# A banded attention and gated scan kernel on one core: a new due-time list schedule, copies moved from DMA to engines, weights loaded on 128 partitions, a second PSUM home for the finals

## The chip, the cores and the metric

The kernel runs on one core of one Trainium2 chip. The metric is the device time of one execution, in microseconds (us). A run here is one execution; medians and ranges are over several. A run is called slow when it is over 1.5% above the fastest of the same kernel, and comparisons use fast runs. Before: 215.98 us median of 4 runs (215.73 to 220.17, the last a slow run) in the comparison with the changed kernel.

Engine names in the profile: PE is TensorE (PEld its weight loads), DVE is VectorE, ACT is ScalarE, POOL is GpSimd, SP is SyncE, which here issues all DMAs but one of 2 KB from one queue (SPq), one after another in its timeline.

## The reference, cut to what matters

```python
# q, k, v: 8 batches x 8 heads x 576 x 64, f32
scores = (q @ k.T) / 8                       # only |i - j| <= 32 counts
attn   = softmax(where(band, scores, -1e9))
x      = heads_side_by_side(attn @ v)        # 8 x 576 x 512
proj   = x @ w_in                            # w_in 512 x 1024
val, gate = proj[..., :512], proj[..., 512:]
for t in range(576):                         # a scan along the sequence
    h = exp(A_log)[0] * h + val[:, t];  ys[:, t] = h
out = (gate * sigmoid(gate) * ys) @ w_out    # w_out 512 x 512
```

## The kernel before

The kernel cuts the 4608 rows (8 x 576) into 9 chunks of 512. Each chunk has 4 attention steps (one for each pair of heads, so 36 steps), then 4 `val` and 4 `gate` projections with scan, tanh, silu and fuse, then 4 finals. The names below return in the profile: `sc` scores, `probs` exp and mask, `pv` probabilities times v, `xT` the transposed attention output, `pjv` and `pjg` the projections, `h` the scan, `fu` the product, `fo` a final, `osb` its eviction (the copy out of PSUM, the memory that the matmuls here write), `tr` the transposes of q and k. I call the PSUM buffer that a result goes to its home.

Nothing is ordered by hand. A small list scheduler, run while the program is written, has a duration and a due time for each of 818 pieces. It picks the engine that can start first and on it, among the pieces that could start within a slack, the one with the earliest due time:

```python
TAU = 4.0
PENALTY = {("pool", "dve"): 1.0, ("pool", "act"): 1.2, ("act", "dve"): 0.3, ("dve", "pool"): 1.0}
SLACK = 0.3
# ... cut: place(k) gives the earliest start and the engine of a piece
while ready:
    cand = [(p[1], ops[k][2], k, p) for k in ready for p in [place(k)] if p]
    cand.sort(key=lambda x: x[0])
    s0, _, _, p0 = cand[0]
    _, _, k, (_, s, d, e) = min((x for x in cand if x[3][3] == p0[3] and x[0] <= s0 + SLACK),
                                key=lambda x: x[1])
    # ... cut: bookkeeping
    emit(e)

# a due time, by a hand-made pattern of 4 us a step:
add(("norm", t), do_norm, dict(dve=0.95), t0 + TAU + 1.2, [("P", t)], opens=[("x16", t)], uses=[("pv", t)])
```

v is needed twice: in blocks that start at even multiples of 64 (`vE`) and at odd ones (`vO`), which is `vE` with the two halves of the partitions exchanged. From the third batch on `vO` is filled by two DMAs from SBUF to SBUF. The weights `w_in` come in by DMAs of 64 partitions each, since that gives the row order that `xT` has:

```python
def shift_v(b, half):
    E, O = vEs[b % 3], vOs[b % 3]
    if half == 0:
        nc.sync.dma_start(out=O[0:64].rearrange("p e h d -> p (e h d)"),
                          in_=E[64:128, 0:4].rearrange("p e h d -> p (e h d)"))
    else:
        nc.sync.dma_start(out=O[64:128].rearrange("p e h d -> p (e h d)"),
                          in_=E[0:64, 1:5].rearrange("p e h d -> p (e h d)"))

src = moe_w_in.rearrange("(s f d) (g c) -> s d f g c", s=2, f=4, g=2)
for s in range(2):
    for g in range(2):
        eng.dma_start(out=t[64 * s:64 * s + 64, :, g, :], in_=src[s, :, :, g, 256 * i:256 * i + 256])

def final(c, tt):
    fo = ps.tile([128, 2, 512], f32, tag="sc", name="fo", bufs=1)[:, 0, :]   # one PSUM home, shared with sc
```

The program keeps one PSUM buffer each for `tr`, `sc` and `pv`, and one of half that size each for `pjv` and `pjg`; finals borrow that of `sc`.

The softmax here doesn't subtract the row's maximum and nothing guards it: scores larger than these inputs give would overflow.

Of the kernel before, what the change touches and what calls it, by code (L numbers as in the profile page):

```python
# [12 lines left out]
TAU = 4.0  # L13
PENALTY = {("pool", "dve"): 1.0, ("pool", "act"): 1.2, ("act", "dve"): 0.3, ("dve", "pool"): 1.0}


def p_all(ns, b, batches):
    return [t for t in range(ns) if b >= 0 and b in batches(t // 4)]


class Sched:
# [4 lines left out]
    def __init__(self):  # L26
        self.ops, self.bufs, self.users = {}, {}, {}
# [4 lines left out]
    def add(self, key, emit, engines, due, deps, opens=(), uses=(), lock=0, mode=None, dma=0.0):  # L32
        self.ops[key] = (emit, engines, due, deps, opens, lock, mode, dma)
        for u in {*opens, *uses}:
            self.users.setdefault(u, []).append(key)

    def run(self):
        ops, users = self.ops, self.users
        left = {k: len(set(o[3])) for k, o in ops.items()}
        after = {}  # L40
        for k, o in ops.items():
            for d in set(o[3]):
                after.setdefault(d, []).append(k)
# [3 lines left out]
        self.log = []  # L47

        def place(k):
            emit, engines, due, deps, opens, lock, m, dma = ops[k]  # L50
            t = max([end[d][0] + (0.12 if end[d][1] != "pe" else 0.2) for d in deps if not (dma and ops[d][7])], default=0.0)
            for u in opens:
                o, n = opened[u[0]], self.bufs[u[0]]
                if len(o) >= n:
                    for x in users[o[len(o) - n]]:
                        if x not in end:
                            return None
                        t = max(t, end[x][0] + 0.1)
            best, first = None, next(iter(engines))
            for e, d in engines.items():  # L60
                s = max(t, free.get(e, 0.0))
                if lock and e in ("dve", "pool") and port[1] != e:
                    s = max(s, port[0])
                if e == "pe" and m != mode[0]:
                    d = d + 0.095
                c = s + d + (PENALTY.get((first, e), 0.0))
                if best is None or c < best[0]:
                    best = (c, s, d, e)
            return best

        while ready:
            cand = [(p[1], ops[k][2], k, p) for k in ready for p in [place(k)] if p]
            cand.sort(key=lambda x: x[0])
            s0, _, _, p0 = cand[0]
            _, _, k, (_, s, d, e) = min((x for x in cand if x[3][3] == p0[3] and x[0] <= s0 + SLACK),
                                        key=lambda x: x[1])
            emit, engines, due, deps, opens, lock, m, dma = ops[k]
            ready.remove(k)
            free[e] = s + d
            end[k] = (s + d, e)  # L80
            if e == "pe":
                mode[0] = m
            if lock and e in ("dve", "pool"):
                port[:] = [s + d, e]
            if dma:
                chan[0] = max(chan[0], s + 0.3) + dma
                end[k] = (chan[0] + 1.2, e)
                free[e] = max(s + d, chan[0] - 6.0)
            for u in opens:
                opened[u[0]].append(u)  # L90
            self.log.append((s, d, e, k))
            emit(e)
            for n in after.get(k, ()):
                left[n] -= 1
                if not left[n]:
                    ready.append(n)
        assert len(end) == len(ops)


SLACK = 0.3  # L100

# [3 lines left out]
def kernel(  # L105
# [23 lines left out]

    stage = {}  # L130
# [21 lines left out]
    def load_w(i, eng):  # L152
        t = T([128, 4, 2, 256], f32, "w32", bufs=2)
        src = moe_w_in.rearrange("(s f d) (g c) -> s d f g c", s=2, f=4, g=2)
        for s in range(2):
            for g in range(2):
                eng.dma_start(out=t[64 * s:64 * s + 64, :, g, :],
                              in_=src[s, :, :, g, 256 * i:256 * i + 256])
        stage["w", i] = t

    def cast_w(i, j):
        t = stage["w", i]
        for g in range(2):
            c0 = 512 * g + 256 * i + 128 * j
            nc.gpsimd.tensor_scalar(
                out=w_in16[:, :, c0:c0 + 128], in0=t[:, :, g, 128 * j:128 * j + 128],
                scalar1=1.0, scalar2=1.0, op0=ALU.mult, op1=ALU.mult)
# [6 lines left out]
    def cast_wo(a):  # L174
        nc.gpsimd.tensor_scalar(out=w_out16[:, 2 * a:2 * a + 2, :], in0=stage["wo"][:, 2 * a:2 * a + 2, :],
                                scalar1=0.5, scalar2=1.0, op0=ALU.mult, op1=ALU.mult)
# [43 lines left out]
    def cast(en, o, i):  # L220
        if en == "act":
            nc.scalar.activation(o, i, AF.Copy, bias=0.0, scale=1.0)  # L222
        elif en == "dve":
            nc.vector.tensor_copy(o, i)  # L224
        else:
            nc.gpsimd.tensor_scalar(out=o, in0=i, scalar1=1.0, scalar2=1.0, op0=ALU.mult, op1=ALU.mult)
# [4 lines left out]
    def shift_v(b, half):  # L231
        E, O = vEs[b % 3], vOs[b % 3]
        if half == 0:
            nc.sync.dma_start(out=O[0:64].rearrange("p e h d -> p (e h d)"),
                              in_=E[64:128, 0:4].rearrange("p e h d -> p (e h d)"))
        else:
            nc.sync.dma_start(out=O[64:128].rearrange("p e h d -> p (e h d)"),
                              in_=E[0:64, 1:5].rearrange("p e h d -> p (e h d)"))
# [117 lines left out]
    def final(c, tt):  # L356
        fo = ps.tile([128, 2, 512], f32, tag="sc", name="fo", bufs=1)[:, 0, :]
# [23 lines left out]
    def eng(e):  # L381
        return {"dve": nc.vector, "act": nc.scalar, "pool": nc.gpsimd, "sp": nc.sync}[e]

# [4 lines left out]
    for k, n in dict(k32=4, q32=4, k16=2, q16=2, w32=2, tr=1, sc=1, pv=1, pjv=1, pjg=1, probs=2, x16=2,  # L388
                     xT=2, th=2, silu=2, fu=2, osb=4, h0=2, h1=2, h2=2, h3=2).items():
        tag(k, n)  # L390
# [18 lines left out]
    prev = None  # L409
    for i, k in enumerate(order):  # L410
        due = 0.01 * i
        deps = [prev] if prev else []
        if k[0] == "ld":
            _, b, g, n = k
            due = max(due, TAU * (4 * b + 2 * g - 9))
            add(k, lambda en, b=b, g=g, n=n: load_qk(b, g, n, nc.sync), dict(sp=0.5), due, deps,
                opens=[(n + "32", b, g)], dma=2.0)
        elif k[0] == "ldv":
            _, b, e = k
            due = max(due, TAU * (4 * b - 8))  # L420
            deps += [("ve", b - 2, j) for j in range(5)] + [("vo", b - 2, j) for j in range(4) if b < 4] if b > 1 else []
            add(k, load_e(b, e), dict(sp=0.5), due, deps, dma=1.2)
        elif k[0] == "ldw":
            add(k, lambda en, i=k[1]: load_w(i, nc.sync), dict(sp=2.0), due, deps, opens=[("w32", k[1])], dma=3.5)
        else:
            add(k, lambda en: load_wo(), dict(sp=0.5), due, deps, opens=[("w32", 2)], dma=3.5)
        prev = k

    for i in range(2):
        for j in range(2):  # L430
            add(("cw", i, j), lambda en, i=i, j=j: cast_w(i, j), dict(pool=1.3), TAU * (4 + i), [("ldw", i)],
                uses=[("w32", i)], lock=1)
        add(("cwo", i), lambda en, i=i: cast_wo(i), dict(pool=1.1), TAU * 7, [("ldo",)], uses=[("w32", 2)], lock=1)
    for cc in range(4):
        add(("arep", cc), lambda en, cc=cc: prep_a(cc), dict(act=1.0), TAU * 3.5 + 0.1 * cc, [("exp", 1)])
    add(("arep0",), lambda en: nc.vector.memset(arep[:, :, 512:513], 0.0), dict(dve=0.1), TAU * 4,
# [4 lines left out]

    for b in range(B):
        for g in range(2):
            for o, n in enumerate("kq"):
                k, t0 = (b, g, n), TAU * (4 * b + 2 * g - 2 + o)
                add(("c",) + k, lambda en, k=k: cast_qk(*k, en), dict(pool=1.25, dve=0.8, act=1.15),
                    t0 - 2 * TAU, [("ld",) + k], opens=[(n + "16", b, g)], uses=[(n + "32", b, g)], lock=1)

                def do_T(en, k=k):
                    live[("tr",) + k] = trans(*k)  # L450

                add(("T",) + k, do_T, dict(pe=0.28), t0 + 0.3, [("c",) + k], opens=[("tr",) + k],
                    uses=[(n + "16", b, g)], mode="row")
                add(("E",) + k, lambda en, k=k: evac(k[0], k[1], live.pop(("tr",) + k), k[2]), dict(act=1.1),
                    t0 + 1.2, [("T",) + k] + ([("S", t) for t in s_steps(b - 2, g)] if b > 1 else []),
                    uses=[("tr",) + k])
        for e in range(5):
            add(("ve", b, e), lambda en, b=b, e=e: cast_v(b, e, e + 1, en), dict(pool=0.65, dve=0.45, act=0.6),
                TAU * (4 * b - 4 + 0.7 * e), [("ldv", b, e)] + ([("P", t) for t in p_all(NS, b - 3, batches)]), lock=1)
# [118 lines left out]
```

## Time and profile before

| | before |
|---|---|
| median of 4 runs | 215.98 us |
| profiled span | 216.7 us |
| TensorE busy | 166.7 us |
| last load of q landed | 146.1 us |
| exp of steps 10, 11, 12 (from 1) | 55.0, 76.0, 79.1 us |

The profiled run took 218.62 us, 2.6 us more than the median. It counts as fast, but all times within this trace come from a long run.

The profile page of the kernel before: span, busy time of each engine, then the span in 40 equal slices (each digit is tenths of busy time; PEclk is the granted TensorE clock), then the chain of work that ended last, by engine.

```profile
span 216.7 us, 5582 instructions
PE 166.7 (77%) x2304; PEld 88.3 (41%) x2304; DVE 131.4 (61%) x217; ACT 140.9 (65%) x190; POOL 115.6 (53%) x126
...
PE   0215649885398478999898999978999999999851
...
PEclk9999999998569958999999999996999999999999
DMA  5999999988999999998998998998112122122232
...
PE 37%; DMA 32%; SPq 12%; ACT 7%; DVE 4%; POOL 4%; issue 3%; POOLq 1%; ACTq 0%; DVEq 0%
```

The DMA row is full up to slice 28 (150 us) and nearly empty after it; the PE row has holes up to about slice 16 (90 us).

Busy time of each engine in three stretches of the kernel before (columns: stretch, its length, PE, PEld, DVE, ACT, POOL busy with the number of instructions, granted clock, DMA share, GB/s):

```profile
0.00:20.00 20.00, 3.75 (x109) 3.22 (x111) 4.74 (x30) 11.85 (x15) 12.27 (x20) 1.00 1.01 228
20.00:90.00 70.00, 50.07 (x756) 28.31 (x752) 38.33 (x59) 46.04 (x57) 47.58 (x53) 0.88 1.00 254
90.00:216.70 126.70, 112.91 (x1447) 56.78 (x1446) 88.33 (x129) 83.01 (x119) 55.77 (x54) 0.99 0.58 175
```

TensorE idles 16.3, 19.9 and 13.8 us in them (length less busy).

The timeline of TensorE in the kernel before (start, length, instruction; in brackets the idle time before it and what ended it):

```profile
58.21 0.66 PE L251 MATMUL tr<-ident,k_892 64*128 64x64 f16 x18 [3.27 <-POOL k_892 L226]
58.81 0.61 PE L310 MATMUL pv<-ident,x_915 128*128 128x128 f16 x4
59.21 1.91 PE L359 MATMUL fo<-w_out_64,fu 128*128 128x512 f16 x4
60.92 1.91 PE L324 MATMUL pjv<-xT,w_in_63 128*128 128x512 f16 x4
...
64.20 1.02 PE L324 MATMUL pjv<-xT,w_in_63 128*128 128x512 f16 x4
...
75.53 0.22 PE L292 MATMUL pv<-vO_94,probs 128*64 128x65 f16 x1 [3.06 <-DMA vO_94<-vE_91]
```

And SyncE's queue at that time:

```profile
53.15 10.72 SPq L144 DMA_DIRECT2D v_1_68<-in_v_dram  x5
...
65.13 0.53 SPq L234 DMA_DIRECT2D vO_94<-vE_91  x1
```

`vO` for batch 3 is issued at 65.1 us, behind five v loads that held the queue for 10.7 us, and TensorE waits for it until 75.5 us. The first four lines show something else: four matmuls of a projection take 1.91 us at 60.9 us and 1.02 at 64.2. The clock records of this trace give 0.5 from 52.6 to 62.9, 76.5 to 83.4 and 148.2 to 151.6 us. These stretches last 10.2, 6.8 and 3.4 us. The three stretches in the windows view (columns as above):

```profile
52.60:62.90 10.30, 6.49 (x74) 3.55 (x76) 3.06 (x6) 4.26 (x6) 8.61 (x10) 0.50 1.08 298
76.50:83.40 6.90, 5.72 (x94) 3.88 (x96) 4.06 (x8) 4.65 (x6) 4.90 (x5) 0.51 0.91 169
148.20:151.60 3.40, 3.40 (x24) 1.40 (x23) 2.90 (x6) 1.90 (x3) 1.47 (x1) 0.50 0.82 248
```

The last finals of the kernel before:

```profile
208.05 1.02 PE L359 MATMUL fo<-w_out_64,fu 128*128 128x512 f16 x4 [0.69 <-ACT osb L222]
209.81 1.02 PE L359 MATMUL fo<-w_out_64,fu 128*128 128x512 f16 x4 [0.73 <-ACT osb L222]
```

With one home each final waits for the eviction of the one before.

### The profile page before, as it was taken

How to read it: one execution, taken by the hardware profiler on the slowest of the kernel's cores; microseconds unless marked ns; L12 is line 12 of the kernel's file. 1: busy time of each engine (PE TensorE's matmuls, PEld its weight loads, DVE VectorE, ACT ScalarE, POOL GpSimd, SP SyncE). 2: the span in 40 equal slices, each digit the busy share in tenths (PEclk: the TensorE clock that was granted, in tenths of full speed). 3: DMA queues.
4: the chain of work that ended last, by engine and by line, in shares of the span. 5: the costliest groups of instructions: out<-in, count | busy, mean ns of one | idle time of the engine just before them, and what ended most of it. 6: DMA issues, size and time to landing. Idle time of an engine off the chain costs nothing.

```text
span 216.7 us, 5582 instructions
## 1 busy us (share of the span) xinstructions
PE 166.7 (77%) x2304; PEld 88.3 (41%) x2304; DVE 131.4 (61%) x217; ACT 140.9 (65%) x190; POOL 115.6 (53%) x126
## 2 busy tenths in 40 slices
PE   0215649885398478999898999978999999999851
PEld 0104534434234254444545545443555444444310
DVE  5004354568328464677598968846787888876600
ACT  2498897747356175688958777756679576644521
POOL 7653672599879663563758493764222423324410
PEclk9999999998569958999999999996999999999999
DMA  5999999988999999998998998998112122122232
GB/s 140 261 296 216 273 270 224 317 201 221 375 167 273 284 178 263 281 263 224 318 343 191 257 342 214 253 294 279 52 50 99 48 77 74 48 97 97 100 142 101
DMA packets 55609, 44.45 MB, mean 205 GB/s; under 512 B 39456, under 2 KB 41504, under 8 KB 55584
## 3 DMA queue, kind: packets, MB, share of 16 engines
q1 hardware_dynamic: 55056, 44.10, 74.6%
q8 instruction: 18, 0.29, 0.6%
q10 hardware_dynamic: 528, 0.00, 0.1%
q14 instruction: 7, 0.06, 0.1%
HBM read 31.46 MB, written 9.44 MB: 189 GB/s over the span
## 4 chain that ended last, share of the span: by engine, by line
PE 37%; DMA 32%; SPq 12%; ACT 7%; DVE 4%; POOL 4%; issue 3%; POOLq 1%; ACTq 0%; DVEq 0%
PE fo L359 10%; PE pjv L324 9%; PE pjg L324 8%; SPq L144 8%; DMA q_1096<-in_q_dram 6%; DMA w_466<-in_moe_w_in_dram 5%; DMA v_1_68<-in_v_dram 4%; DMA vO_92<-vE_89 4%; DMA out_dram<-osb 4%; DMA w_180<-in_moe_w_in_dram 3%; PE pv L292 3%; DMA vO_93<-vE_90 3%; ACT probs L278 3%; PE sc L269 3%; DMA k_775<-in_k_dram 3%
## 5 line engine op out<-in xcount | busy, mean ns | idle before, releaser
L278 ACT ACTIVATE probs<-sc 128x1024 f16<-128x1024 f32 x36 | 36.9, 1025 | 12.4 <-PE pv L292 7.9
L359 PE MATMUL fo<-w_out_64,fu 128*128 128x512 f16 x144 | 39.3, 396 | 4.7 <-ACT osb L222 2.8
L324 PE MATMUL pjv<-xT,w_in_63 128*128 128x512 f16 x144 | 39.6, 400 | 0.6 <-DVE h_1093 L333 0.5
L324 PE MATMUL pjg<-xT,w_in_63 128*128 128x512 f16 x144 | 38.8, 393 | 0.0
L222 ACT ACTIVATE osb<-fo 128x512 f32<-128x512 f32 x34 | 20.3, 597 | 27.1 <-PE fo L359 22.8
L324 PEld LDWEIGHTS <-w_in_63 128*128 128x128 f16 x288 | 25.6, 100 | 28.5 <-issue 5.6
L283 DVE TENSOR_TENSOR probs<-probs,mask 128x1024 f16<-128x1024 f16 x36 | 27.5, 766 | 14.8 <-ACT probs L278 14.5
L345 DVE SCALAR_TENSOR_TENSOR silu<-th,pjg 128x512 f16<-128x512 f16 x36 | 24.6, 685 | 18.2 <-ACT th L340 17.6
L340 ACT ACTIVATE th<-pjg 128x512 f16<-128x512 f32 x36 | 21.5, 596 | 13.8 <-PE pjg L324 13.5
L359 PEld LDWEIGHTS <-fu 128*128 128x128 f16 x144 | 13.8, 101 | 22.4 <-issue 9.9
L292 PEld LDWEIGHTS <-probs 128*64 128x64 f16 x576 | 14.7, 120 | 15.9 <-issue 10.5
L222 ACT ACTIVATE xT<-pv 128x512 f16<-128x512 f16 x28 | 16.7, 596 | 5.0 <-PE pv L310 4.6
L300 DVE RECIPROCAL rc<-pv 128x8 f32<-128x8 f32 x36 | 7.2, 200 | 15.3 <-PE pv L292 15.3
L269 PE MATMUL sc<-qT_0_81,kT_0_85 64*128 64x64 f16 x144 | 5.6, 207 | 8.2 <-ACT probs L278 5.6
L292 PE MATMUL pv<-vE_89,probs 128*64 128x65 f16 x120 | 10.5, 212 | 1.0 <-DVE xT L224 0.5
L292 PE MATMUL pv<-vE_90,probs 128*64 128x65 f16 x120 | 10.1, 203 | 0.3 <-ACT xT L222 0.3
L292 PE MATMUL pv<-vO_94,probs 128*64 128x65 f16 x64 | 6.5, 212 | 3.4 <-DMA vO_94<-vE_91 3.1
L292 PE MATMUL pv<-vO_92,probs 128*64 128x65 f16 x96 | 8.7, 216 | 0.1
L292 PE MATMUL pv<-vO_93,probs 128*64 128x65 f16 x96 | 8.2, 203 | 0.3
L256 ACT ACTIVATE kT_0_85<-tr 128x1152 f16<-128x1152 f16 x4 | 4.5, 1132 | 5.7 <-PE tr L251 5.7
L269 PEld LDWEIGHTS <-kT_0_85 64*128 64x128 f16 x144 | 4.3, 105 | 9.8 <-issue 9.2
L292 PE MATMUL pv<-vE_91,probs 128*64 128x65 f16 x80 | 7.1, 209 | 0.1
(337 smaller groups left out, 327.2 us busy)
## 6 DMA issues: line engine op xcount, KB each, us to landing
out_dram<-osb SPq DMA_DIRECT2D x36, 256.0 KB, 2.4
v_0_67<-in_v_dram SPq DMA_DIRECT2D x12, 256.0 KB, 8.1
v_1_68<-in_v_dram SPq DMA_DIRECT2D x12, 256.0 KB, 9.0
v_0_67<-in_v_dram SPq DMA_DIRECT2D x8, 192.0 KB, 6.5
v_1_68<-in_v_dram SPq DMA_DIRECT2D x8, 192.0 KB, 7.5
vO_94<-vE_91 SPq DMA_DIRECT2D x4, 260.0 KB, 8.9
vO_92<-vE_89 SPq DMA_DIRECT2D x4, 260.0 KB, 8.0
vO_93<-vE_90 SPq DMA_DIRECT2D x4, 260.0 KB, 5.2
```

The source lines that it names most:

```text
L144: eng.dma_start(out=v32s[b % 2][p0:p1, e], in_=v[b, :, lo + p0:lo + p1, :].rearrange("h p d -> p h d"))
L222: nc.scalar.activation(o, i, AF.Copy, bias=0.0, scale=1.0)
L256: nc.scalar.activation(dst.rearrange("p x (m j) -> p x m j", j=9), tr[:, :, 0:576].rearrange("p x (j m) -> p x m j", j=9), AF.Copy, bias=0 ...
L269: nc.tensor.matmul(out=sc[:, h, 64 * r:64 * r + 64], lhsT=kTs[hp][b % 2][64 * h:64 * h + 64, 64 * i:64 * i + 128], rhs=qTs[hp][b % 2][64 * ...
L278: nc.scalar.activation(pr, sc, AF.Exp, bias=0.0, scale=1.0 / 8.0)
L283: nc.vector.tensor_tensor(out=pr, in0=pr, in1=m[:, None, :].to_broadcast([128, 2, 512]), op=ALU.mult)
L292: nc.tensor.matmul(out=pv[p0:p0 + 64, h, 65 * (r // 2):65 * (r // 2) + 65], lhsT=pr[:, h, 64 * r:64 * r + 64], rhs=vt, start=True, stop=True)
L300: nc.vector.reciprocal(rc, view[:, :, :, 64])
L324: nc.tensor.matmul(out=pj, lhsT=w_in16[:, fc, 128 * oc:128 * oc + 128], rhs=xT[c][:, fc, :], start=(fc == 0), stop=(fc == 3))
L340: nc.scalar.activation(th, pj, AF.Tanh, bias=0.0, scale=0.5)
L345: nc.vector.scalar_tensor_tensor(out=si, in0=th, scalar=1.0, in1=pj, op0=ALU.add, op1=ALU.mult)
L359: nc.tensor.matmul(out=fo, lhsT=fu[c][:, cc, 128 * tt:128 * tt + 128], rhs=w_out16[:, cc, :], start=(cc == 0), stop=(cc == 3))
```

## The change

Its intent: to find a better order by searching the due times offline against the scheduler's own model, to take the copies into `vO` off the DMA queue, to load `w_in` at full width, and to let finals alternate between the home of the scores and that of the transposes. The core of the diff:

```diff
-PENALTY = {("pool", "dve"): 1.0, ("pool", "act"): 1.2, ("act", "dve"): 0.3, ("dve", "pool"): 1.0}
+DUE = dict(c=13.9, T=0.98, E=-2.61, ve=63.57, sh=1.66, S=0.23, exp=4.28, mask=0.36, P=3.47, norm=-6.44,
+           X=6.42, xe=8.54, val=7.86, scan=1.95, gate=7.94, tanh=4.27, silu=-3.88, fuse=11.92, fin=11.72,
+           fe=0.01, st=-9.32)
+SLACK = 0.24
+SAME_MODE = 0
+LEAVE = dict(pool_dve=-0.1, pool_act=-0.13, act_dve=0.62, dve_pool=2.14, dve_act=-2.01, act_pool=-0.11)
...
+        due = {k: TAU * o[2][0] + DUE.get(o[2][1], 0.0) for k, o in ops.items()}
...
-        src = moe_w_in.rearrange("(s f d) (g c) -> s d f g c", s=2, f=4, g=2)
-            for g in range(2):
-                eng.dma_start(out=t[64 * s:64 * s + 64, :, g, :],
-                              in_=src[s, :, :, g, 256 * i:256 * i + 256])
+        src = moe_w_in.rearrange("(a p) (g c) -> p a g c", p=128, g=2)
+        for g in range(2):
+            eng.dma_start(out=t[:, :, g, :], in_=src[:, :, g, 256 * i:256 * i + 256])
+    # cast_w: four casts of 64 partitions, which put the rows in xT's order (was two of 128)
...
-    def shift_v(b, half):          # two DMAs
+    def shift_v(b, half, en):      # VectorE or GpSimd
+        o, i = (O[0:64], E[64:128, 0:4]) if half == 0 else (O[64:128], E[0:64, 1:5])
+        cast(en, o.rearrange("p e h d -> p (e h d)"), i.rearrange("p e h d -> p (e h d)"))
...
-        fo = ps.tile([128, 2, 512], f32, tag="sc", name="fo", bufs=1)[:, 0, :]
+        fo = ps.tile([128, 2, 512], f32, tag=sch.tag_of["fo", c, tt], name="fo", bufs=1)[:, 0, :]
+    sch.either["fo"] = ("sc", "tr")
...
-            [("mask", t)] + [("ve", b, e) for b in batches(c) for e in range(5)]
-            + [("vo", b, e) if b < 2 else ("sh", b, e // 2) for b in batches(c) for e in range(4)],
+            [("mask", t)] + list(v_tiles(c)),     # only the v tiles that this chunk reads
```

Cut: casts of weights may now go to any of three engines, some of the scheduler's durations are refined, and one rule of its choice on TensorE (`SAME_MODE`) is new.

## The prediction

> **What bounds the kernel now.** Two stages. Up to about 90 us, the DMA system: the 40-slice row shows the DMA engines at 90% or more from 5 to 150 us, and the chain of waits is almost only DMA before 91 us (w_in 7.5 and 11.9, v 8.8, q 12.3, vO 8.3 us). TensorE is busy 45 of the 70 us from 20 to 90 (busy time by windows). After 92 us the chain is nearly all TensorE, busy 92% of 90 to 140 and over 97% of 150 to 200 us. An attention step takes 3.9 us at the end (exps from 158.8 to 186.3 us, seven steps), 4.5 us on average from 83.6 us on. Between the exps at 55.0 and 76.0 us there is a hole: the P matmuls wait for vO, a DMA copy issued only at 65.1 (its input landed at 54.0, its casts ended at 56) because it stood in SyncE's queue behind v loads; it landed at 74.6 and 75.5.
>
> **What is removed.** Packet times summed, over 16 engines: q/k 60 us, v (256-byte packets) 49, vO copies 11.6, w_in 11.0, stores and w_out 28.5. The copies (3.2 MB) go. The w_in packets of 1 KB cost 86 ns, as much as 2 KB ones (89), with 64 partitions a transfer; on 128 partitions I estimate about 5 of the 11 us saved. So the loads should finish 14 to 17 us earlier (before: last q at 146 us). [...]
>
> **What is added.** Twelve copies of 64x2080 f16 on DVE or POOL. [...] Scaled from the 512-element POOL cast (0.62 us): 2.2 to 2.5 us on POOL. The w_in casts double to 16 half-partition casts, about 0.6 us each on POOL (+5 us). [...] ACT 3.8, TensorE about 4.2 with transposes: tight, TensorE still first.
>
> **What moves.** Finals may use the bank of the transposes: waits of finals and scores on osb evictions (2.8 + 2.3 us) shrink. The first exps need not stand behind 5.2 us of vO casts on ACT. P waits only for the v tiles it reads.
>
> **On the critical path.** Of some 25 us that TensorE idles from 20 to 90 us I expect 12 to 15 back, about 3 from the start, 1 to 2 from finals and late DMA waits; the last 65 us, TensorE at its limit plus a serial tail of finals, keep their length. 216 - 17 = 199 us.
>
> **Right if:** the hole after the exp at 55 us is gone; the last q lands near 131 us; TensorE busy time stays at 160 to 168 us while its share rises to 82 to 86%; the last exp comes near 169 us; no DMA writes vO.
>
> **Wrong if:** the granted clock (0.5 from 52.6 to 62.9 and 76.5 to 83.4 us) falls more often under a denser TensorE; DVE becomes the limit, or shares badly with POOL; the searched due times fit a model that the chip does not follow; or (faster) the order saves TensorE waits after 90 us too.
>
> Predicted 199 us, range 191 to 208. Chances: faster 0.93, within 2% 0.05, slower 0.02.

12 to 15, about 3 and 1 to 2 came to the 17 of 216 - 17 = 199 us. That the loads finish 14 to 17 us earlier remains as the author's estimate, from the packet times and the full DMA row. So do the 5 us for `w_in`: packets of 1 KB at half the 89 ns of 2 KB ones would save 5.3 of the 11.0 us; that the number of partitions sets the cost was not shown then.

## More of the kernel before

PEclk falls in three places. A trap: it shows 9 in the first seven slices too, where the trace has no clock record at all (the first begins at 39.0 us), while the matmuls there take the slow time (the 16 scores of a step 0.61 us, later 0.41).

In the 3.4 us before each of the three falls TensorE was busy 1.35, 0.41 and 1.53 us, and in the 3.4 us before each of the three rises 3.40, 3.20 and 3.40.

## The result, and the profile after

The changed kernel takes 192.91 us median of 4 runs (192.12 to 193.43). The ratio to the kernel before is 0.893 (0.889 to 0.897). Ratios are the mean time of one kernel's fast runs over that of the other's of the same rounds, so not quite the ratio of the medians. That is inside the predicted range, 6 us below the predicted 199.

The profile page of the changed kernel:

```profile
span 191.4 us, 5578 instructions
PE 155.4 (81%) x2304; PEld 84.5 (44%) x2304; DVE 160.0 (84%) x252; ACT 149.7 (78%) x203; POOL 100.0 (52%) x98
...
PE   0221577796856998999899998999999999999991
...
PEclk9999999999999999999999999999999999999999
DMA  5999999998999959998997999961112121122255
...
PE 49%; DVE 25%; ACT 15%; issue 5%; DMA 3%; SPq 0%; ACTq 0%
```

DMA and SyncE's queue, 44% of the chain before, are 3% of it; VectorE is now a quarter. TensorE runs the same 2304 matmuls in 11.3 us less busy time. The same three stretches of the changed kernel:

```profile
0.00:20.00 20.00, 4.02 (x112) 3.30 (x114) 10.80 (x41) 12.83 (x15) 4.17 (x11) 1.00 1.00 261
20.00:90.00 70.00, 57.08 (x977) 32.34 (x974) 62.19 (x93) 61.03 (x80) 40.59 (x41) 1.00 1.00 272
90.00:191.40 101.40, 94.32 (x1225) 48.82 (x1222) 87.02 (x120) 75.88 (x111) 55.26 (x47) 1.00 0.52 167
```

Idle is 16.0, 12.9 and 7.1 us. So the span's 25.3 us are 14.0 us less idle (0.3 + 7.0 + 6.7) and 11.3 us less busy time. The busy part: the trace has no slow clock between 40.9 and 191.1 us. Before 40.9 us it has no clock record, and matmuls take the slow time (four of a projection 1.91 us at 38.3, 1.03 at 41.0); TensorE was busy 17.3 of the 30 us from 10 to 40. In the kernel before, TensorE was busy 15.6 us inside its three slow stretches (by the windows of those stretches); half of that, 7.8 us, is my estimate of what the slow clock added to busy time in this run, which was a long one. The rest of the 11.3 us is not taken apart; ends of matmuls are modelled, and a group that stands alone looks longer than one in a row (1.02 against 0.90 us for four of 512 columns).

How much of the 7.8 us the whole time felt is not shown. Three signs speak against booking all of it. The step with the slow stretch from 148.2 us takes 5.2 us (exps 27 to 28), and 5.3 in b_copies_engines (below), which has no slow clock there. Of the four runs of the changed kernel the fastest (192.12 us) has the lowest mean clock, 0.990 (0.010 of its 190.2 us, so about 3.8 us at half clock). And two fast runs of the kernel before on one chip took 214.94 us at a mean clock of 0.941 and 216.01 at 0.968.

The copies into `vO`, and two places on VectorE's timeline of the changed kernel with GpSimd's beside them. First the group (mean in ns after the busy time), then VectorE, then GpSimd:

```profile
L245 DVE COPY vO<-vE 64x2080 f16<-64x2080 f16 x12 | 13.5, 1123 | 0.4
```

```profile
91.54 2.27 DVE L245 COPY vO<-vE 64x2080 f16<-64x2080 f16 x2
```

```profile
91.60 1.66 POOL L371 TENSOR_TENSOR fu<-h,silu 128x512 f16<-128x512 f32 x1 [0.59 <-DVE silu L362]
93.23 2.08 POOL L247 TENSOR_SCALAR vE<-v 128x512 f16<-128x512 f32 x2
```

```profile
105.77 0.70 DVE L245 COPY vO<-vE 64x2080 f16<-64x2080 f16 x1
```

Alone, at 105.8 us, a copy takes 0.70 us. Of the pair at 91.5 us the first took 0.70 and the second 1.56, and GpSimd's `fu`, 1.15 to 1.16 us in 32 of 36 cases before (1.47 to 1.60 in the other four), took 1.66 (in the whole changed kernel 22 of its 35 took 1.16 at most, the others 1.47 to 1.66). So in this trace instructions of both engines took longer where the two overlapped, though not all: the first copy had `fu` beside it for all but its first 0.06 us. The second copy ended 0.56 us after `fu` did. Why is not shown.

The last finals after: six of them, back to back, 0.9 us each in place of 1.75 apart.

```profile
181.85 5.38 PE L376 MATMUL fo<-w_out,fu 128*128 128x512 f16 x24
```

### The profile page after: what moved, and what is told of

It is laid out like the page before. It is cut to its first block, busy times and chain, and to the rows that moved or that the text cites. A ratio compares the mean times of both kernels' runs of the same rounds, so it can differ in the third digit from the quotient of the medians.

```text
span 191.4 us, 5578 instructions
## 1 busy us (share of the span) xinstructions
PE 155.4 (81%) x2304; PEld 84.5 (44%) x2304; DVE 160.0 (84%) x252; ACT 149.7 (78%) x203; POOL 100.0 (52%) x98
## 4 chain that ended last, share of the span: by engine, by line
PE 49%; DVE 25%; ACT 15%; issue 5%; DMA 3%; SPq 0%; ACTq 0%
PE fo L376 12%; PE pjg L341 12%; PE pjv L341 11%; DVE h L350 5%; DVE vO L245 5%; DVE probs L300 5%; PE pv L309 5%; ACT probs L295 4%; DVE x L319 4%; PE tr L268 4%; DMA q<-in_q_dram 3%; PE sc L286 3%; PE pv L327 3%; DVE silu L362 2%; ACT kT L273 2%
## 5 line engine op out<-in xcount | busy, mean ns | idle before, releaser
L371 POOL TENSOR_TENSOR fu<-h,silu 128x512 f16<-128x512 f32 x35 | 45.6, 1303 | 54.2 <-DVE silu L362 49.3
L350 DVE TENSOR_TENSOR_SCAN h<-arep,h,pjv 128x512 f32<-128x512 f32 x32 | 40.8, 1276 | 3.5 <-PE pjv L341 3.4
L341 PE MATMUL pjv<-xT,w_in 128*128 128x512 f16 x144 | 39.2, 394 | 2.2 <-DVE h L350 1.5
L341 PEld LDWEIGHTS <-w_in 128*128 128x128 f16 x288 | 25.9, 99 | 29.8 <-issue 5.4
L341 PE MATMUL pjg<-xT,w_in 128*128 128x512 f16 x144 | 37.9, 387 | 0.6 <-DVE silu L362 0.6
L376 PE MATMUL fo<-w_out,fu 128*128 128x512 f16 x144 | 36.3, 380 | 0.4 <-ACT osb L243 0.3
L247 POOL TENSOR_SCALAR vE<-v 128x512 f16<-128x512 f32 x29 | 22.3, 780 | 23.7 <-DMA v<-in_v_dram 23.7
L357 ACT ACTIVATE th<-pjg 128x512 f16<-128x512 f32 x36 | 21.5, 598 | 14.2 <-PE pjg L341 13.5
L319 DVE TENSOR_TENSOR x<-pv,rc 128x512 f16<-128x512 f32 x36 | 24.9, 691 | 1.2
L273 ACT ACTIVATE kT<-tr 128x1152 f16<-128x1152 f16 x16 | 18.0, 1126 | 4.9 <-PE tr L268 4.8
L273 ACT ACTIVATE qT<-tr 128x1152 f16<-128x1152 f16 x16 | 18.1, 1131 | 4.0 <-PE tr L268 4.0
L309 PEld LDWEIGHTS <-probs 128*64 128x64 f16 x576 | 13.5, 116 | 16.4 <-issue 14.5
```

The source lines that it names most:

```text
L247: eng(en).tensor_scalar(out=o, in0=i, scalar1=scale, scalar2=1.0, op0=ALU.mult, op1=ALU.mult)
L273: nc.scalar.activation(dst.rearrange("p x (m j) -> p x m j", j=9), tr[:, :, 0:576].rearrange("p x (j m) -> p x m j", j=9), AF.Copy, bias=0 ...
L309: nc.tensor.matmul(out=pv[p0:p0 + 64, h, 65 * (r // 2):65 * (r // 2) + 65], lhsT=pr[:, h, 64 * r:64 * r + 64], rhs=vt, start=True, stop=True)
L319: nc.vector.tensor_tensor(out=x, in0=view[:, :, :, 0:64], in1=rc[:, :, :, None].to_broadcast([128, 4, 2, 64]), op=ALU.mult)
L341: nc.tensor.matmul(out=pj, lhsT=w_in16[:, fc, 128 * oc:128 * oc + 128], rhs=xT[c][:, fc, :], start=(fc == 0), stop=(fc == 3))
L350: nc.vector.tensor_tensor_scan(out=h, data0=arep[:, cc, 512 - 64 * c:1024 - 64 * c], data1=pj, initial=init, op0=ALU.mult, op1=ALU.add)
```

## The experiments

I split each span at two landmarks, the start of the 13th exp and of the 29th, read from the list of the 36 exps in each trace. The first stretch is where loads set the pace (DMA share 1.00 or 1.01 up to 90 us in the kernel before), the second is the middle, the third is the rest with the tail of finals. The landmarks follow the attention steps and not all work: of the 432 matmuls with 512 columns (projections and finals) the middle holds 185 in the kernel before, 179 in the changed kernel, 170 in s_old_parts and 164 in s_all. One of them takes about 0.22 us in a row, so a few us of a shorter middle can be work moved out of it. "Old dues" are the due times, slack and penalties of before; "searched" means searched for that very program; all rows but the first two use the new scheduler. All runs gave correct results.

| kernel | copies | w_in on | homes | dues | median us (range) | 13th exp at | 13th to 29th | 29th to end |
|---|---|---|---|---|---|---|---|---|
| before | DMA | 64 | 1 | old | 215.98 (215.73 to 220.17) | 83.6 | 75.2 | 57.9 |
| b_copies_engines | engines | 64 | 1 | old | 212.81 (212.45 to 214.63) | 76.0 | 76.6 | 58.1 |
| a_old_dues | engines | 128 | 2 | old | 207.0 (205.61 to 208.46) | 76.0 | 75.4 | 53.0 |
| s_old_parts | DMA | 64 | 1 | searched | 207.25 (206.12 to 207.62) | 79.0 | 68.8 | 56.2 |
| s_all | engines | 128 | 2 | searched | 195.35 (195.08 to 195.55) | 71.4 | 66.4 | 55.9 |
| s_one_home | engines | 128 | 1 | searched | 197.52 (197.13 to 198.78) | 71.8 | 68.7 | 54.7 |
| s_copies_dma | DMA | 128 | 2 | searched | 198.51 (196.15 to 199.81) | 73.3 | 67.5 | 55.7 |
| s_copies_dma_2 | DMA | 128 | 2 | searched | 197.15 (195.73 to 201.5) | 70.2 | 69.0 | 55.9 |
| changed | engines | 128 | 2 | given | 192.91 (192.12 to 193.43) | 68.1 | 67.5 | 55.8 |
| a_one_home | engines | 128 | 1 | given | 207.25 (206.34 to 207.93) | 67.2 | 78.9 | 59.1 |
| a_weights64 | engines | 64 | 2 | given | 193.03 (192.19 to 195.9) | 67.8 | 68.0 | 55.5 |
| a_copies_dma | DMA | 128 | 2 | given | 214.11 (212.73 to 219.05) | slow run | | |

The last three columns are from the profiled run, the median from all runs, four or more each. Kernels of different calls ran on different chips; the kernel before ran beside each of them, its fast runs at 213.2 to 216.9 us. One run each of s_copies_dma (199.81), s_copies_dma_2 (201.5) and a_weights64 (195.9), and two of a_copies_dma, were slow. Each row has one trace, so a landmark can be off by the 2 or 3 us by which runs of one kernel differ.

### First theory: the copies; rival: the due times

My theory was that of the prediction: the DMA copies made the hole and took DMA time, so they are most of the gain. The rival: the searched order is.

**b_copies_engines**: the kernel before with the copies on engines, alone.

```diff
-        nc.sync.dma_start(out=O[0:64]..., in_=E[64:128, 0:4]...)    # and the other half
+        cast(en, o.rearrange("p e h d -> p (e h d)"), i.rearrange("p e h d -> p (e h d)"))
-    add(("sh", b, h), ..., dict(sp=0.5), ..., dma=0.7)
+    add(("sh", b, h), ..., dict(dve=0.75, pool=2.1), ..., lock=1)
```

> The kernel before with one part of the change alone: the twelve copies into vO run on VectorE or GpSimd instead of as DMAs; due times, weights and homes as before. Theory C (the copies: 11.6 us of DMA-engine time, and the wait in SyncE's queue behind blocked v loads, made the hole of the scores between 55 and 76 us, and the hole made TensorE's clock fall to half): 203 to 208 us, no exp-to-exp gap over 15 us, half-clock windows in the middle gone or shorter. Rival S (the searched due times do most of it, the copies little): 212 us or more.

Measured: 212.81 us, ratio 0.989 (0.978 to 1.000). The hole is gone: exps at 51.9, 59.0, 62.2, 71.3 and 76.0 us, so the 13th comes 7.6 us earlier. A slow clock stays (13.7 us from 52.9, against 17.1 in the first two stretches before). But the middle is no faster (76.6 us). The lead in the traces is down to 2.4 us at the 21st exp (115.7 against 118.1) and 6.0 at the end, part of which is the long profiled run of the kernel before; fast runs of the same call differ by 2.6 us in the mean. The removed wait is real, and about 3 us of it are left in the time. The hole was 21 us between two exps, but TensorE had other work in it: it stood idle for `vO` for 3.1 us (the line at 75.53 us above). The time is the rival's (212 or more); that no gap between exps exceeds 15 us is what my theory said.

**a_copies_dma**: the changed kernel with the copies as DMAs from SyncE, each at the same place of the order.

```diff
-        cast(en, o.rearrange("p e h d -> p (e h d)"), i.rearrange("p e h d -> p (e h d)"))
+        nc.sync.dma_start(out=o.rearrange("p e h d -> p (e h d)"), in_=i.rearrange("p e h d -> p (e h d)"))
```

> The changed kernel with one part undone: the same order of everything, but each of the twelve copies into vO is a DMA from SyncE's queue at the same place of the order. Theory C: 199 to 207 us, a hole of some 10 us in the scores, half clock after it. Rival S: 192 to 195 us, as VectorE even gets 13.5 us of work less.

Measured: 214.11 us (212.73 to 219.05), ratio 0.990, so all the gain is lost, more than either theory said. The profile (of a slow run, 217.3 us; used here only for where it waits and what follows): TensorE's timeline, then the list of waits.

```profile
62.41 0.26 PE L309 MATMUL pv<-vO,probs 128*64 128x65 f16 x1 [8.59 <-DMA vO<-vE]
...
62.94 1.89 PE L341 MATMUL pjv<-xT,w_in 128*128 128x512 f16 x4
```

```profile
PE pv L309 <- DMA vO<-vE: 25.3, 5, 8.6
```

An order made for copies of 0.7 to 1.5 us meets DMAs that land 3.1 to 9.3 us after issue, five times, and after the hole of 8.6 us matmuls go at half speed (four of a projection 1.89 us at 62.9, 1.02 at 52.3 before it; mean granted clock 0.79 from 60 to 80 us). This shows that the order and the copies belong together, not what the copies are worth.

**a_old_dues**: the changed kernel with the due times of before.

```diff
-DUE = dict(c=13.9, T=0.98, ...)   SLACK = 0.24   LEAVE = dict(pool_dve=-0.1, ...)
+DUE = dict(c=-8.0, T=0.3, E=1.2, ve=-16.0, sh=-6.0, S=0.0, exp=0.4, mask=1.5, P=4.6, norm=5.2,
+           X=6.7, xe=7.1, val=1.0, scan=2.0, gate=3.0, tanh=3.95, silu=4.6, fuse=5.3, fin=1.9,
+           fe=2.9, st=3.5)
+SLACK = 0.3
+LEAVE = dict(pool_dve=1.0, pool_act=1.2, act_dve=0.3, dve_pool=1.0, dve_act=0.0, act_pool=0.0)
```

> The changed kernel with the due times, the slack and the penalties for leaving the first engine of before (copies on engines, weights on 128 partitions and two homes stay). Theory C: 195 to 200 us. Rival S: 205 us or more.

Measured: 207.0 us, ratio 0.960 (0.947 to 0.973). The rival's number: all parts and the rest of the new scheduler, without the search, are worth about 9 us, and the middle takes 75.4 us as before. So 16 steps take about 4.7 us each with the old dues whatever moves the copies, and 4.2 with the given ones in the program that they were searched for.

**a_one_home**: the finals in one home again.

```diff
-    sch.either["fo"] = ("sc", "tr")
+    sch.either["fo"] = ("sc",)
```

> The changed kernel with the finals in the bank of the scores alone. Theory C: 193 to 196 us, most of it at the last finals, which in the trace of before stood 0.7 us apart for an eviction each, and in the trace after do not. Rival H (the second home is what keeps TensorE at 98% from 130 us on): 199 us or more.

Measured: 207.25 us, ratio 0.961. As TensorE's timeline shows, each of the last finals waits for an eviction again:

```profile
198.73 1.02 PE L376 MATMUL fo<-w_out,fu 128*128 128x512 f16 x4 [0.73 <-ACT osb L243]
200.48 1.02 PE L376 MATMUL fo<-w_out,fu 128*128 128x512 f16 x4 [0.73 <-ACT osb L243]
```

Its number is that of the rival. But the tail is only 3 of the 14 us; the middle grew from 67.5 to 78.9 us, though the clock never fell between 40.4 and 204.2 us in this trace. Taken alone this run says that the second home is worth 14 us, and taken alone a_copies_dma says that the copies are worth 21. With a_old_dues that would be about 50 us out of 23 (14.3, 21.2 and 14.1). My reading, tested next: undoing a part also breaks the fit of the due times to the program.

### Second theory: fit

So the theory became: due times searched for one program are wrong for its neighbour, and a part can only be weighed with due times searched anew for each program. I wrote a search of my own (random changes of the 21 due offsets, slack and penalties, accepted as in annealing, about 70,000 tries against the scheduler's model) and ran it for each variant. Rival: the parts are worth what undoing them costs.

**a_weights64**: `w_in` in the way of before, same order of everything.

```diff
-        for g in range(2):
-            eng.dma_start(out=t[:, :, g, :], in_=src[:, :, g, 256 * i:256 * i + 256])
+        for s in range(2):
+            for g in range(2):
+                eng.dma_start(out=t[64 * s:64 * s + 64, :, g, :], in_=src[s, :, :, g, 256 * i:256 * i + 256])
     # and two casts of 128 partitions in place of four of 64
```

> The changed kernel with w_in loaded on 64 partitions a transfer (four DMAs a half) and cast by two instructions, in the same order of everything. By packet sums of the two traces this costs 11.0 against 6.3 us of DMA-engine time (86 against 49 ns a packet of 1 KB). Theory D (loads are what the first 60 us wait for): 195 to 198 us. Rival E (in the first 60 us VectorE and ScalarE are as full as the DMAs, so the loads have room): 192 to 194.5 us.

Measured: 193.03 us (ratio 0.893), the same as the changed kernel. The packets of 1 KB cost 86 ns before and 49 after, 11.0 against 6.3 us of DMA-engine time in the two traces of before and after, and it is worth nothing here. This undoing broke no fit; its trace has one slow stretch (50.4 to 53.8 us), and that run (192.97 us) took no longer than those of the changed kernel. The time doesn't need the cheaper packets.

**s_one_home, s_old_parts, s_all**: due times searched anew for one home; for all three parts as before; and, as a control of my search, for all parts as changed, starting from the old dues. The edits are those of above and the constants.

> One home for the finals as in a_one_home (207 us), but with due times that I searched anew for that program (some 70,000 tries against the scheduler's own model of the chip). Theory F (fit: undoing a part costs much because the due times were searched for the program with that part; a new search gets it back): 195 to 200 us. Rival P (the second home itself is worth 14 us): 205 us or more.

> All three parts as before (copies by DMA, w_in on 64 partitions, one home), planned as such by the new scheduler with due times searched anew. If the search alone can do the work, 200 us or less. If the DMA copies in SyncE's in-order queue limit any order, 204 us or more, with TensorE idle before matmuls that read vO and half clock after that.

> Control of my own search: all parts as in the changed kernel, due times searched by the same method and as long, starting from those of before (a_old_dues, 207 us). Theory F: 195 to 200 us, as near s_one_home as 2 us. Rival P: 10 us or more below s_one_home.

Measured: 197.52, 207.25 and 195.35 us (ratios 0.916, 0.959 and 0.904). One home costs 2.2 us, not 14: fit holds. The old parts with a searched order gain 8.7 us over before. The traces, which differ by 12.7, put 4.6 of it before the 13th exp, 6.4 in the middle (68.8 us, with 15 large matmuls fewer in it) and 1.7 after. They are 11.9 us behind s_all, 7.6 of it before the 13th exp. The time is what I expected if the DMA copies limit any order. But that expectation named idle before matmuls that read `vO`: the longest in the trace is 1.8 us and all of it 3.3, so that mechanism is not what holds it back. Busy windows of s_all and of a_old_dues, in this order, which differ in due times, slack and penalties (`SAME_MODE` among them) alone:

```profile
20.00:90.00 70.00, 55.75 (x997) 32.62 (x997) 54.91 (x86) 63.04 (x80) 50.93 (x53) 1.00 1.03 282
90.00:193.70 103.70, 95.15 (x1206) 49.03 (x1204) 86.68 (x122) 75.39 (x108) 48.16 (x44) 1.00 0.49 157
```

```profile
20.00:90.00 70.00, 52.55 (x862) 29.45 (x855) 45.84 (x70) 58.06 (x77) 48.22 (x51) 0.95 1.02 286
90.00:204.40 114.40, 104.00 (x1342) 53.37 (x1340) 90.00 (x127) 80.86 (x118) 53.11 (x49) 0.97 0.44 139
```

By 90 us s_all has run 997 matmuls of these 20 to 90 us, a_old_dues 862.

**s_copies_dma** and **s_copies_dma_2**: copies by DMA, planned as DMAs, due times searched anew from two random starts.

> Copies into vO by DMA again, the other two parts as changed, planned as such, due times searched anew as for s_all (195.4 us) and s_one_home (197.5 us). Old parts with a new search took 207.3 us; with the second home worth about 2 us and the weights nothing, theory C2 (the DMA copies are what is left of the difference, about 9 us, for they load the DMA engines and hold up SyncE's queue): 202 to 207 us. Rival F2 (a good order hides the DMA copies too): 199 us or less.

> A second search result for the same program as s_copies_dma (copies by DMA, the rest as changed; 198.5 us), from another random start; the scheduler's model puts it 1.7 us behind the first. It tells how much of a few us between searched kernels is luck of the search: luck below 2 us if it takes 197 to 201 us; more if it lies outside.

Measured: 198.51 and 197.15 us (ratios 0.919 and 0.915). So a good order hides most of the DMA copies too; the fast runs are 197.7 and 196.7 us in the mean, 2.4 and 1.3 us above the 195.3 of s_all. These are other chips than that of s_all; by the ratios to the kernel before it is 3.3 and 2.3 us. The luck of the search is of that size. A first search result for this program was left out, as its order deadlocked when it was built. All three parts undone cost 11.9 us, the two that cost something 3.5 to 5.5 when undone singly (2.2, and 1.3 to 3.3). I did not settle whether they add up to more than their sum or whether my one search for s_old_parts, which was given a dearer `w_in` load in its model, ended early.

### Two tries for more

**a_warm**: idle matmuls to bring the clock up early.

```diff
+        if b < 2:
+            spare = tr[:, 0, 640:896].bitcast(f32)
+            for _ in range(56 if (b, g, n) == (0, 0, "k") else 16):
+                nc.tensor.matmul(out=spare, lhsT=ident, rhs=ident, start=True, stop=True)
```

> The changed kernel with idle matmuls added (identity times identity into an unused part of the transposes' bank): 56 before the first transposes, 16 before each of the next seven. In the trace after, TensorE's matmuls take twice as long until 40.9 us (16 scores 0.61 us, later 0.41; val 1.91, later 1.04). Theory W (the slow clock of the first 41 us is on the critical path): full clock before 20 us and 189 to 191 us. Rival N (in the first 41 us ScalarE, VectorE and loads set the pace, TensorE has room): the clock rises early, but 192 to 194 us.

Measured: 197.73 us, slower than the changed kernel, which neither theory had. TensorE's timeline:

```profile
1.42 5.96 PE L268 MATMUL tr<-ident 128*128 128x128 f16 x56 [1.42 <-POOL ident masks.py:199]
7.32 0.44 PE L272 MATMUL tr<-ident,k 64*128 64x64 f16 x18
...
14.52 1.89 PE L268 MATMUL tr<-ident 128*128 128x128 f16 x16
```

The clock rose at 7.0 us, and the transposes took 0.44 us in place of 0.66. It fell at 13.9 us, after 3.4 us in which TensorE was busy for 0.4, and stayed down to 34.4 (and twice more, from 37.8 and from 65.1, for 3.4 us). From then each group of 16 idle matmuls took 1.9 us ahead of real work, and the ninth exp came 4.7 us later (55.7 against 51.0). So TensorE's queue does stand on the path in this stretch, but whether a full clock there helps is open: this run had one from 7.0 to 13.9 and from 34.4 to 37.8 us alone. The profiled run was a long one (199.45 us).

**best_n**: the decay factors `arep` filled by any engine, from one small exp, `vO` casts of the first two batches on GpSimd too, due times and offsets of single pieces searched anew.

```diff
-        nc.scalar.activation(arep[:, cc, :], a_log[:, cc:cc + 1].to_broadcast([128, 1024]), AF.Exp, ...)
+        cast(en, arep[:, cc, :], a_exp[:, cc:cc + 1].to_broadcast([128, 1024]))
-             dict(act=1.0), (3.5 + 0.05 * cc, "S"), [("exp", 1)])
+             dict(pool=1.1, act=1.05, dve=1.1), (3.5 + 0.05 * cc, "arep"), [], lock=1)
```

> A try for a faster kernel. As the changed one, but the decay factors (4.0 us of broadcasts on ScalarE in the first 20 us of the trace after, ahead of the evacuation of the next keys) may be filled by GpSimd, which idles then; the vO casts of the first two batches may go to GpSimd as well; due times and small offsets for single instructions searched anew, with two sets of costs disturbed by up to 8% beside the model's own. Theory G (the first 30 us are held up by ScalarE): 188 to 191 us. Rival (the order of the changed kernel was at the end of what this kind of search gives): 192 to 196 us.

Measured: 197.67 us, ratio 0.917, worse than the changed kernel and than the rival. The search put the fills first, at 6.3 us, on VectorE and ScalarE, where the small exp had just waited for its load (6.0 us); the first transposes start at 9.2 us and not 6.0, and the slow clock came back three times (13.6 us in all). The model that is searched knows neither that load's landing nor the clock. No kernel of mine beats the changed one.

## Why the prediction was right or wrong

- **The time.** 199 us was predicted, 191 to 208; 192.9 was measured. The direction and the range were right, and faster at 0.93 was right. The explanation under the number was right only in part, so that the total landed in the range is partly luck: busy time that I had not counted made up for idle time that did not come back.
- **The idle time.** I wrote that TensorE was busy 45 of the 70 us from 20 to 90 us; the windows give 50.1, an error of my addition. I expected 16 to 20 us of idle back, and 14.0 came back, but elsewhere: 7.0 us from 20 to 90 (predicted 12 to 15), 0.3 at the start (predicted 3), 6.7 after 90 us (predicted 1 to 2). At 90 us, though, the changed kernel is further on in its work. Counted by landmarks, it is 15.5 us ahead at the 13th exp (about half of it idle and half busy time, and with 11 of the large matmuls, about 2.4 us, put off), which is near what I had predicted for the first stage; it gains 7.7 us more in the middle and 2.1 after, where I had predicted 1 to 2.
- **The step that failed**: "TensorE busy time stays at 160 to 168 us". It fell to 155.4. That term was set at zero and measured 11.3 us. I read the half clock before as something that might strike more often under a denser TensorE. The traces show the reverse: it came after thin activity (in the 3.4 us before each fall TensorE was busy 0.4 to 1.5 us in the kernel before and 0.4 before the fall at 13.9 us in a_warm), and in the profiled run it went when the holes went (1.00 from 40.9 to 191.1 us). I estimate it at about 7.8 of the 11.3 us of busy time.
- **"The last 65 us ... keep their length"**: nearly so. From the 29th exp to the end it was 57.9 us before and 55.8 after; the finals no longer stand 1.75 us apart. The gain that I missed lies ahead of it, in the middle, where 16 steps went from 75.2 to 67.5 us. I took 4.5 us a step as set by DMA and TensorE; b_copies_engines shows that removing DMA work alone leaves it as it was, and s_old_parts that a searched order with the old parts (and the new scheduler) shortens it to 68.8. Which waits of the middle the order removes is not shown.
- **The credit given to the copies.** I put most of the gain down to them. Alone they gave about 3 us with the old dues, and with a fitted order they are worth 1 to 3. The hole itself was read rightly; that ending it would carry through to the end was not.
- **What held.** No DMA writes `vO`; the last q landed at 128.4 us (predicted 131); the `w_in` packets saved 4.7 us of DMA-engine time (predicted 5), though a_weights64 shows that it was worth nothing; a copy takes 0.70 us alone. Twelve of them took 13.5 us and not the 8.4 of twelve at 0.70, for those that met GpSimd took up to 1.56.
- **Signs that missed.** The last exp came at 162.2 us, not 169. The gap after the exp at 55 us shrank from 21.0 to 11.3 us and was not gone (exps at 52.7 and 64.0); TensorE has other work in it. TensorE's share is 81%, a little under the 82 to 86 predicted.

Where the 23 us came from, as far as it is shown: two comparisons change one thing within the new scheduler. The search alone (a_old_dues to s_all) gives 11.7 us, and the three parts together, each side with its own search (s_old_parts to s_all), give 11.9. Against the kernel before, the searched order with the old parts gives 8.7 us, the new parts with the old dues 9.0, and both 20.6; these three also hold the rest of the new scheduler. The last 2.4 us, from s_all to the changed kernel, are due times from a better search. Why the parts are worth 11.9 together and at most 5.5 singly stays open.

## What to carry to other kernels

When all engines are nearly full, an order searched for one program is part of that program. Undoing one part with its due times kept measured 14 and 21 us for parts worth 1 to 3 (and nothing for the weights), so weigh a part with the order fitted anew. A hole on TensorE has two sides in the trace of the kernel before: the idle time (3.1 us before the line at 75.53 us), and matmuls at half speed after it (clock 0.5 from 76.5 to 83.4 us). Look for both when a change removes one, but do not book the second as time before a run shows it. A wait that is removed early pays only as far as the stages after it keep the lead: of 7.6 us about 3 were left in b_copies_engines.
